# Queries and keys of the later pairs loaded in 32 by 32 blocks and turned by the vector engine instead of TensorE, in a fused attention and SwiGLU kernel

## The chip, the cores and the metric

One core of a Trainium2 chip; the four sets of experiments ran on four different chips, each with the kernel before beside it. The time is the device time of one execution in microseconds; quoted are medians of repeated runs with their lowest and highest. All runs of this study were in the fast state (granted TensorE clock 0.994 to 0.998 of full speed in the profiled ones). Profiled spans are some 2 us shorter than the times, and their sums are told as spans. One profile is of one run, and runs of one kernel differ by up to some 4 us, so differences of spans are checked against medians where it matters.

## The reference, cut to what matters

```python
# q, k, v: (8 batches, 12 heads, 448 tokens, 64 features), fp32
def rmsnorm(x, g):
    rms = np.sqrt(np.mean(x * x, axis=-1, keepdims=True) + 1e-06)
    return x / rms * g
q_n, k_n = rmsnorm(q, g_q), rmsnorm(k, g_k)
scores = np.matmul(q_n, k_n.transpose(0, 1, 3, 2)) / np.sqrt(64)
attn = softmax(scores)                          # rows of 448
out = np.matmul(attn, v)
# then (8*448, 768) tokens go through a SwiGLU block: w_gate, w_val 768x1536, w_out 1536x768
```

In both kernels the products of the scores take queries and keys with features on partitions. They come from memory with tokens first: somebody has to turn (transpose) them.

## The kernel before

Two heads make a pair; there are 48 pairs. Pairs 0 to 11 run first and are not touched. Pairs 12 to 47 are woven into the SwiGLU block's products in three stretches of twelve. Every piece of work is registered with an engine, an estimated duration, a wished time and its dependencies; a list scheduler then fixes the order of instructions of each engine. The timelines below show ScalarE in that order: in the changed kernel its exponentials start at 776.11 us, behind a copy that waits for the vector engine until 775.54 (3.4 us after TensorE's first scores of the pair; 2.6 us in e13, where that copy comes sooner). Pieces marked `port=True` are kept apart in the scheduler's plan; in the piece of code below these are the scalings and the additions of the sums, but not the power. The names of PSUM (where TensorE's results lie) and SBUF (the working memory) are used as in the code.

```python
BUFS = dict(qk=4, v=2, t=2, QT=2, KT=2, e=4, eh=2, ..., st=2, at=2, ss=3, rr=4, ...)   # cut

def attention(m):                    # one later pair
    # load: tokens on partitions, rows of 64 features (256 B), 8 issues a pair   (cut)
    def summed():                    # squares were made by ScalarE into t
        ss = take("ss", m, [P, 2 * 2 * NJ])
        nc.vector.tensor_reduce(out=ss, in_=..., axis=AX.X, op=ALU.add)   # 16 norms a partition
        nc.vector.tensor_scalar_add(ss, ss, D * 1e-6)
    def inverse():                   # 1/sqrt as a power, on GpSimd
        nc.gpsimd.tensor_tensor(out=rr, in0=tiles["ss", m], in1=minus_half, op=ALU.pow)
    # scale(x): t = qk * rr on GpSimd, once for queries and once for keys, port=True   (cut)
    def transpose():                 # 8 TensorE transposes into a PSUM tile
        ps = take("st", (m, "t"), [P, 2, TB])
        for x in range(2):
            for j in range(NJ):
                w = width(j)
                nc.tensor.transpose(ps[:, x, ds(P * j, w)], ..., ident[0:w, 0:w])
    def keys():                      # PSUM -> SBUF
        nc.scalar.copy(take("KT", m, [P, S]), tiles["st", (m, "t")][:, 1, 0:S])
    def queries():                   # PSUM -> SBUF, times both gains
        nc.vector.tensor_scalar(out=take("QT", m, [P, S]), in0=tiles["st", (m, "t")][:, 0, 0:S],
                                scalar1=gg, scalar2=None, op0=ALU.mult)
    # scores: QT, KT -> st;  exps on ScalarE: st -> e
    # sums of exps: two GpSimd additions (add_up 1, 2), then the last part on the vector engine:
    adds.append(add("DVE", 1.24, base + 6.0, lambda: add_up(3), after=[ex[3], adds[-1]], port=True, ...))
    # weighted sums (e, v -> at) and denominators (ones x sums -> st) on TensorE   (cut)
```

Of the kernel before, what the change touches and what calls it, by code (L numbers as in the profile page):

```python
# [9 lines left out]
F32 = mybir.dt.float32  # L10
# [459 lines left out]
def fast(  # L470
# [39 lines left out]
    P = 128  # L510
# [24 lines left out]
        qk=4, v=2, t=2, QT=2, KT=2, e=4, eh=2, sums=1, more=1, inv=1, rows=3, st=2, at=2, ss=3, rr=4,  # L535
# [41 lines left out]
    minus_half = const.tile([P, 2 * 2 * NJ], F32, name="minus_half")  # L577
# [36 lines left out]
    def first_attention(m):  # L614
# [57 lines left out]
        def inverse():  # L672
            rr = take("rr", m, [R, 2 * 2 * NJ])
            nc.gpsimd.tensor_tensor(
                out=rr,
                in0=tiles["ss", m],
                in1=minus_half[0:R],
                op=ALU.pow,
            )
# [178 lines left out]

    def width(j):
        return P if j < NJ - 1 else D  # L860

    def attention(m):
# [13 lines left out]
        def load(name, key, src, when):  # L876
            def emit():
                x = take(name, key, [P, NJ, 2, D])
                for h in range(2):
                    rows = src[b, 2 * c + h][0 : P * (NJ - 1)]  # L880
                    nc.sync.dma_start(x[:, 0 : NJ - 1, h], rows.rearrange("(j p) d -> p j d", p=P))
                rows = src[b][2 * c : 2 * c + 2, P * (NJ - 1) :].rearrange("h s d -> s h d")
                for p in (0, D):
                    nc.sync.dma_start(x[ds(p, D), NJ - 1], rows)

            return add("SP", 2.4, when, emit, takes=[(name, key)], kb=256, early=25.0)

        loaded = [load("qk", (m, x), src, ready - 26.0) for x, src in enumerate((q, k))]
        load_v = load("v", m, v, ready - 16.0)

        def square(x):
            if x == 0:
                take("t", m, [P, 2, NJ, 2, D])
            nc.scalar.activation(
                tiles["t", m][:, x].rearrange("p j h d -> p (j h d)"),
                tiles["qk", (m, x)].rearrange("p j h d -> p (j h d)"),
                AF.Square,
            )

        squares = []  # L900
        for x in range(2):
            squares.append(
                add(
                    "ACT", 0.6, ready - 15.0, lambda x=x: square(x),
                    after=[loaded[x], *squares], uses=[("qk", (m, x))] + [("t", m)] * x,
                    takes=[("t", m)] * (1 - x),
                )
            )

        def summed():  # L910
            ss = take("ss", m, [P, 2 * 2 * NJ])
            nc.vector.tensor_reduce(
                out=ss, in_=tiles["t", m].rearrange("p x j h d -> p (x j h) d"), axis=AX.X, op=ALU.add
            )
            nc.vector.tensor_scalar_add(ss, ss, D * 1e-6)  # L915

        sums = add(
            "DVE", 1.4, ready - 14.0, summed, after=squares, uses=[("t", m)], takes=[("ss", m)]
        )

        def inverse():
            rr = take("rr", m, [P, 2 * 2 * NJ])
            nc.gpsimd.tensor_tensor(out=rr, in0=tiles["ss", m], in1=minus_half, op=ALU.pow)  # L923

        rr = add(
            "POOL", 3.0, ready - 12.0, inverse, after=[sums], uses=[("ss", m)], takes=[("rr", m)]
        )

        def scale(x):
            rr = tiles["rr", m][:, ts(x, 2 * NJ)].rearrange("p (n one) -> p n one", one=1)  # L930
            nc.gpsimd.tensor_tensor(  # L931
                out=tiles["t", m][:, x].rearrange("p j h d -> p (j h) d"),
                in0=tiles["qk", (m, x)].rearrange("p j h d -> p (j h) d"),
                in1=rr.to_broadcast([P, 2 * NJ, D]),
# [5 lines left out]
                "POOL", 1.03, ready - 8.0, lambda x=x: scale(x), after=[rr], port=True,  # L940
                uses=[("qk", (m, x)), ("t", m), ("rr", m)],
            )
            for x in range(2)
# [3 lines left out]
        def transpose():  # L947
            ps = take("st", (m, "t"), [P, 2, TB])
            for x in range(2):
                for j in range(NJ):  # L950
                    w = width(j)
                    nc.tensor.transpose(  # L952
                        ps[:, x, ds(P * j, w)],
                        tiles["t", m][0:w, x, j].rearrange("p h d -> p (h d)"),
                        ident[0:w, 0:w],
                    )

        turned = add(
            "PE", 0.9, ready - 6.0, transpose, after=scaled, uses=[("t", m)],
            takes=[("st", (m, "t"))], mode="full",  # L960
        )

        def keys():
            nc.scalar.copy(take("KT", m, [P, S]), tiles["st", (m, "t")][:, 1, 0:S])  # L964

        def queries():
            nc.vector.tensor_scalar(  # L967
                out=take("QT", m, [P, S]), in0=tiles["st", (m, "t")][:, 0, 0:S], scalar1=gg,
                scalar2=None, op0=ALU.mult,
# [3 lines left out]
            "ACT", 0.53, ready - 5.0, keys, after=[turned], takes=[("KT", m)],  # L973
            uses=[("st", (m, "t"))],
        )
        qt = add(
            "DVE", 0.68, ready - 5.0, queries, after=[turned], takes=[("QT", m)],
            uses=[("st", (m, "t"))],
# [730 lines left out]
```

## Time and profile before

| | before |
|---|---|
| time, median of 3 runs | 1597.41 us (1596.78 to 1598.51) |
| profiled span | 1596.5 us |
| TensorE busy | 1558.7 us |
| vector, ScalarE, GpSimd busy | 864.6, 418.5, 661.9 us |
| denominator to denominator inside a stretch | 15.78 us |

The last row is the gauge that this document uses most. Each later pair has one burst on TensorE (scores, weighted sum, scores, denominator) and then matmuls of the SwiGLU block up to the next burst. The eight denominator matmuls (out st, in sums and ones) occur once a pair, so the distance between their starts is the pair's period. A pair whose period is well above the usual one is called late below. One caution: where the scheduler puts the denominators behind half of a product, one period is long and a later one short, and little is lost. The prediction shows the busy line, the chain and the main groups of this kernel.

One view that the prediction does not show: the chain of work near the end of the first stretch of the kernel before (start us, us, what).

```profile
495.39 0.54 ACT KT L964
...
495.95 0.70 DVE QT L967
...
496.69 0.98 PE st L989 x8
```

TensorE ended its turns (L952) at 495.37 and has no product left to put between them and the scores (L989), so the way through PSUM, copy of the keys and then the queries, lies on the chain: 496.69 - 495.37 = 1.32 us of it is not TensorE's.

### The profile page before, as it was taken

To read this page: it belongs to the slowest core of one execution; us is meant where nothing else is said; L and a number is where in the kernel's file an instruction comes from. 1 tells how busy PE (TensorE), PEld (TensorE's weight loads), DVE (VectorE), ACT (ScalarE), POOL (GpSimd) and SP (SyncE) were. 2 spreads that over 40 slices of the span, in tenths; PEclk is the share of its full clock that TensorE was granted. 3 is DMA by queue.
4 is the path that set the end of the run, shared out by engine and by line. 5 is a ranking of instruction groups with operands and counts; after the bars stand their busy time and mean duration, and the time that the engine had idled before them with its cause. 6 is when DMAs were issued, how large, how long until landed. Compare 5 with 4: busy or idle time off the path is not lost.

```text
span 1596.5 us, 17686 instructions
## 1 busy us (share of the span) xinstructions
PE 1558.7 (98%) x6672; PEld 778.3 (49%) x6672; DVE 864.6 (54%) x1017; ACT 418.5 (26%) x617; POOL 661.9 (41%) x440
## 2 busy tenths in 40 slices
PE   6998999999999999999999999999999999999998
PEld 2333544545454555544555455554545455555555
DVE  5989768775565434345556633444565563343221
ACT  6864333233332101122333200112333311000000
POOL 5881447564552322444554322344565331222000
PEclk9999999999999999999999999999999999999999
DMA  6655687643422113222333121332333211111232
GB/s 174 198 158 192 223 269 238 217 128 80 116 66 88 60 40 86 74 87 64 104 106 94 52 70 40 88 77 76 105 98 98 70 65 59 40 60 40 94 109 76
DMA packets 195012, 166.82 MB, mean 104 GB/s; under 512 B 132453, under 2 KB 184933, under 8 KB 194149
## 3 DMA queue, kind: packets, MB, share of 16 engines
q1 hardware_dynamic: 186304, 154.57, 32.3%
q10 hardware_dynamic: 8612, 11.02, 2.0%
q8 instruction: 55, 0.90, 0.2%
q14 instruction: 41, 0.33, 0.1%
HBM read 135.66 MB, written 29.88 MB: 104 GB/s over the span
## 4 chain that ended last, share of the span: by engine, by line
PE 77%; DVE 1%; ACT 1%; issue 0%; ACTq 0%
PE mm L1308 35%; PE mm L1489 25%; PE at L1058 6%; PE st L989 6%; PE st L952 3%; PE st L1071 2%; DVE gt L1420 0%; ACT es L1000 0%; DVE sums L1011 0%; DVE hs L1457 0%; DVE QT L967 0%; ACT wide L1413 0%; DVE gt L1457 0%; DVE s L1326 0%; ACT KT L964 0%
## 5 line engine op out<-in xcount | busy, mean ns | idle before, releaser
L1308 PE MATMUL mm<-xs,ws 128*128 128x448 f32 x2016 | 767.0, 542 | 7.4 <-DVE xs L1145 4.9
L1308 PEld LDWEIGHTS mm<-xs,ws 128*128 128x128 f32 x2016 | 381.9, 190 | 386.4 <-issue 370.9
L1292 POOL TENSOR_TENSOR ws<-ws 128x384 f32<-128x384 f32 x192 | 205.7, 1082 | 419.2 <-DMA ws<-quarters 314.6
L1489 PE MATMUL mm<-ws,gt 128*128 128x384 f32 x912 | 306.9, 491 | 0.0
L1489 PEld LDWEIGHTS mm<-ws,gt 128*128 128x128 f32 x912 | 169.6, 190 | 129.1 <-issue 16.9
L923 POOL TENSOR_TENSOR rr<-ss,minus_half 128x16 f32<-128x16 f32 x36 | 106.8, 2965 | 164.8 <-DVE ss L915 160.6
L1000 ACT ACTIVATE es<-st 128x896 f32<-128x896 f32 x108 | 95.2, 915 | 190.2 <-PE at L1058 141.1
L1005 POOL TENSOR_TENSOR sums<-es 128x896 f32<-128x896 f32 x36 | 76.0, 2112 | 156.6 <-ACT es L1000 120.7
L989 PE MATMUL st<-QT,KT 64*64 64x448 f32 (+1 forms) x1152 | 112.4, 501 | 5.5 <-DVE QT L967 3.5
L1326 DVE TENSOR_TENSOR s<-s,mm 128x448 f32<-128x448 f32 x96 | 59.6, 620 | 105.1 <-PE mm L1308 105.0
L1104 DVE RECIPROCAL inv<-inv 128x448 f32<-128x448 f32 x36 | 106.3, 2953 | 1.2
L1326 DVE TENSOR_TENSOR wide<-s,mm 128x448 f32<-128x448 f32 x72 | 44.7, 620 | 100.3 <-PE mm L1308 100.3
L1489 PE MATMUL mm<-ws,hs 128*128 128x384 f32 x288 | 97.2, 491 | 0.0
L1326 DVE TENSOR_TENSOR gt<-s,mm 128x448 f32<-128x448 f32 x72 | 44.6, 620 | 89.0 <-PE mm L1308 89.0
L1349 ACT COPY s<-mm 128x448 f32<-128x448 f32 x48 | 25.5, 532 | 246.5 <-PE mm L1308 246.5
L1058 PE MATMUL at<-es,v 64*64 64x448 f32 x864 | 89.5, 541 | 0.0
L1110 DVE TENSOR_TENSOR xs<-xs,at 128x448 f32<-128x448 f32 x36 | 22.3, 620 | 123.2 <-ACT xs L1107 123.2
L931 POOL TENSOR_TENSOR t<-qk,rr 128x512 f32<-128x512 f32 x72 | 86.2, 1218 | 2.5
L1413 ACT ACTIVATE wide<-gt 128x1344 f32<-128x1344 f32 x24 | 31.8, 1323 | 182.6 <-DVE gt L1326 182.6
L1005 POOL TENSOR_TENSOR sums<-sums,es 128x896 f32<-128x896 f32 x36 | 75.2, 2090 | 2.7
L1489 PEld LDWEIGHTS mm<-ws,hs 128*128 128x128 f32 x288 | 53.5, 190 | 40.9 <-issue 4.2
L1566 DVE TENSOR_TENSOR rows<-part,mm 128x384 f32<-128x384 f32 x56 | 30.9, 552 | 69.6 <-PE mm L1489 53.7
(93 smaller groups left out, 1374.9 us busy)
## 6 DMA issues: line engine op xcount, KB each, us to landing
ws<-quarters SPq DMA_DIRECT2D x48, 768.0 KB, 4.3
ws<-out_sides SPq DMA_DIRECT2D x28, 1152.0 KB, 6.2
out_sides<-hs SPq DMA_DIRECT2D x6, 1536.0 KB, 7.6
out_dram<-rows ACTq DMA_DIRECT2D x42, 192.0 KB, 1.9
stage<-in_moe_w_val_dram SPq DMA_DIRECT2D x10, 768.0 KB, 6.5
qk<-in_q_dram SPq DMA_DIRECT2D x72, 96.0 KB, 2.6
qk<-in_k_dram SPq DMA_DIRECT2D x72, 96.0 KB, 2.6
v<-in_v_dram SPq DMA_DIRECT2D x72, 96.0 KB, 2.5
```

The costliest lines, as they stand in the source:

```text
L923: nc.gpsimd.tensor_tensor(out=rr, in0=tiles["ss", m], in1=minus_half, op=ALU.pow)
L931: nc.gpsimd.tensor_tensor(out=tiles["t", m][:, x].rearrange("p j h d -> p (j h) d"), in0=tiles["qk", (m, x)].rearrange("p j h d -> p (j h) ...
L952: nc.tensor.transpose(ps[:, x, ds(P * j, w)], tiles["t", m][0:w, x, j].rearrange("p h d -> p (h d)"), ident[0:w, 0:w],)
L989: nc.tensor.matmul(st[ds(D * x, D), h, 0:n], tiles["KT", m][rows, ds(P * j + D * of_keys, D)], tiles["QT", m][rows, ds(Q * of_queries, n)] ...
L1000: nc.scalar.activation(e, tiles["st", (m, j)][:, :, 0 : S * width(j) // P], AF.Exp)
L1005: nc.gpsimd.tensor_tensor(out=to, in0=tiles["e", (m, 0)] if j == 1 else to, in1=e, op=ALU.add)
L1058: nc.tensor.matmul(tiles["at", (m, x)][ds(D * h, D), queries], tiles["v", m][rows, j, h], tiles["e", (m, j)][rows, h], start=j == 0, stop= ...
L1104: nc.vector.reciprocal(inv, inv)
L1292: lambda to=to, a=a, b=b: nc.gpsimd.tensor_tensor(out=tiles[key][:, to], in0=tiles[key][:, a], in1=tiles[key][:, b], op=ALU.subtract,),
L1308: nc.tensor.matmul(into[:, 0:S], w[:, side, c, :], xs[:, side, c], start=(fresh and c == 0), stop=(c == NK - 1), skip_group_check=not fina ...
L1326: nc.vector.tensor_tensor(out=to(), in0=one(), in1=two[:, 0:S], op=ALU.add)
L1489: nc.tensor.matmul(banks[bank][:, 0:HALF], of(g), w[:, ts(g, HALF)], start=(g == 0), stop=(g == NG - 1),)
```

## The change

The intent: take the transposes off TensorE, which is busy for 98% of the span, and give them to the vector engine, which is not. `nc.vector.transpose` is used block by block, 32 by 32: the load places each head's features in two halves of 32, in four partition groups, and each block is turned where it lies (128x448 took 0.62 to 0.64 us, and the result is correct). Each partition then holds half of each row's sum of squares; the halves are swapped by four small copies and added, and the power runs on 28 columns instead of 16.

```diff
-            # rows of 64 features, tokens on partitions
+                to = take("qk", (m, x), [P, NC, C])                  # C = 32, NC = 14
+                for g in range(P // C):
+                    rows = src[b, 2 * c + g // 2][:, ts(g % 2, C)]
+                    nc.sync.dma_start(to[ts(g, C)], rows.rearrange("(c i) f -> i c f", i=C))
...
-            nc.vector.tensor_scalar_add(ss, ss, D * 1e-6)
+        def swap():
+            for g in range(P // C):
+                nc.scalar.copy(ss[ts(g ^ 1, C), 1], ss[ts(g, C), 0])
+        def both():
+            nc.vector.scalar_tensor_tensor(
+                ss[:, 0], ss[:, 0], D * 1e-6, ss[:, 1], op0=ALU.add, op1=ALU.add)
...
-            nc.gpsimd.tensor_tensor(out=rr, in0=tiles["ss", m], in1=minus_half, op=ALU.pow)   # 16
+            nc.gpsimd.tensor_tensor(out=rr, in0=tiles["ss", m][:, 0], in1=minus_half, op=ALU.pow)  # 28
...
-        def transpose():   # 8 x nc.tensor.transpose into PSUM
-        def keys():        # ScalarE, PSUM -> KT
-        def queries():     # vector engine, PSUM -> QT, times gg
+        def transpose(x):
+            to = take("KT", m, [P, S]) if x else tiles["qk", (m, 0)]...
+            nc.vector.transpose(to, tiles["t", m][:, x]...)
+        def queries():
+            nc.scalar.activation(take("QT", m, [P, S]), tiles["qk", (m, 0)]..., AF.Copy, scale=gg)
```

Wished times and estimates of these pieces change with it (the load 2 us earlier, squares and reduction 3, the power 2, the scalings 1, keys before queries); `ss` has two buffers instead of three.

More of the change, by code (lines that the diff above doesn't have):

```diff
@@ L534, in fast @@
     BUFS = dict(
-        qk=4, v=2, t=2, QT=2, KT=2, e=4, eh=2, sums=1, more=1, inv=1, rows=3, st=2, at=2, ss=3, rr=4,
+        qk=4, v=2, t=2, QT=2, KT=2, e=4, eh=2, sums=1, more=1, inv=1, rows=3, st=2, at=2, ss=2, rr=4,
         ws=2, s1=1, s2=1, s3=1, wide=1, part=7,
@@ L576, in fast @@
     gg = const.tile([P, 1], F32, name="gg")
-    minus_half = const.tile([P, 2 * 2 * NJ], F32, name="minus_half")
+    minus_half = const.tile([P, 2 * S // 32], F32, name="minus_half")
     warm = const.tile([P, 1], F32, name="warm")
@@ L676, in inverse @@
                 in0=tiles["ss", m],
-                in1=minus_half[0:R],
+                in1=minus_half[0:R, 0 : 2 * 2 * NJ],
                 op=ALU.pow,
@@ L857, in first_attention @@
             sides(b // 2, c % NK, when + 6.0)
+    C = 32
+    NC = S // C
     def width(j):
@@ L874, in attention, with load, load_values @@
         add = order.add
-        def load(name, key, src, when):
+        def load(x, src):
             def emit():
-                x = take(name, key, [P, NJ, 2, D])
-                for h in range(2):
-                    rows = src[b, 2 * c + h][0 : P * (NJ - 1)]
-                    nc.sync.dma_start(x[:, 0 : NJ - 1, h], rows.rearrange("(j p) d -> p j d", p=P))
-                rows = src[b][2 * c : 2 * c + 2, P * (NJ - 1) :].rearrange("h s d -> s h d")
-                for p in (0, D):
-                    nc.sync.dma_start(x[ds(p, D), NJ - 1], rows)
-            return add("SP", 2.4, when, emit, takes=[(name, key)], kb=256, early=25.0)
-        loaded = [load("qk", (m, x), src, ready - 26.0) for x, src in enumerate((q, k))]
-        load_v = load("v", m, v, ready - 16.0)
+                to = take("qk", (m, x), [P, NC, C])
+                for g in range(P // C):
+                    rows = src[b, 2 * c + g // 2][:, ts(g % 2, C)]
+                    nc.sync.dma_start(to[ts(g, C)], rows.rearrange("(c i) f -> i c f", i=C))
+            return add("SP", 2.4, ready - 28.0, emit, takes=[("qk", (m, x))], kb=224, early=25.0)
+        loaded = [load(x, src) for x, src in enumerate((q, k))]
+        def load_values():
+            x = take("v", m, [P, NJ, 2, D])
+            for h in range(2):
+                rows = v[b, 2 * c + h][0 : P * (NJ - 1)]
+                nc.sync.dma_start(x[:, 0 : NJ - 1, h], rows.rearrange("(j p) d -> p j d", p=P))
+            rows = v[b][2 * c : 2 * c + 2, P * (NJ - 1) :].rearrange("h s d -> s h d")
+            for p in (0, D):
+                nc.sync.dma_start(x[ds(p, D), NJ - 1], rows)
+        load_v = add("SP", 2.4, ready - 16.0, load_values, takes=[("v", m)], kb=256, early=25.0)
         def square(x):
             if x == 0:
-                take("t", m, [P, 2, NJ, 2, D])
-            nc.scalar.activation(
-                tiles["t", m][:, x].rearrange("p j h d -> p (j h d)"),
-                tiles["qk", (m, x)].rearrange("p j h d -> p (j h d)"),
-                AF.Square,
-            )
+                take("t", m, [P, 2, NC, C])
+            nc.scalar.activation(tiles["t", m][:, x], tiles["qk", (m, x)], AF.Square)
         squares = []
@@ L903, in attention @@
                 add(
-                    "ACT", 0.6, ready - 15.0, lambda x=x: square(x),
+                    "ACT", 0.53, ready - 18.0, lambda x=x: square(x),
                     after=[loaded[x], *squares], uses=[("qk", (m, x))] + [("t", m)] * x,
@@ L910, in summed @@
         def summed():
-            ss = take("ss", m, [P, 2 * 2 * NJ])
             nc.vector.tensor_reduce(
-                out=ss, in_=tiles["t", m].rearrange("p x j h d -> p (x j h) d"), axis=AX.X, op=ALU.add
-            )
-            nc.vector.tensor_scalar_add(ss, ss, D * 1e-6)
+                out=take("ss", m, [P, 2, 2 * NC])[:, 0],
+                in_=tiles["t", m].rearrange("p x c f -> p (x c) f"),
+                axis=AX.X,
+                op=ALU.add,
+            )
+        def swap():
+            ss = tiles["ss", m]
+            for g in range(P // C):
+                nc.scalar.copy(ss[ts(g ^ 1, C), 1], ss[ts(g, C), 0])
@@ L917, in attention, with inverse @@
+        def both():
+            ss = tiles["ss", m]
+            nc.vector.scalar_tensor_tensor(
+                ss[:, 0], ss[:, 0], D * 1e-6, ss[:, 1], op0=ALU.add, op1=ALU.add
+            )
+        def inverse():
+            rr = take("rr", m, [P, 2 * NC])
+            nc.gpsimd.tensor_tensor(
+                out=rr, in0=tiles["ss", m][:, 0], in1=minus_half, op=ALU.pow
+            )
         sums = add(
-            "DVE", 1.4, ready - 14.0, summed, after=squares, uses=[("t", m)], takes=[("ss", m)]
+            "DVE", 1.1, ready - 17.0, summed, after=squares, uses=[("t", m)], takes=[("ss", m)]
@@ L919, in attention @@
         )
-        def inverse():
-            rr = take("rr", m, [P, 2 * 2 * NJ])
-            nc.gpsimd.tensor_tensor(out=rr, in0=tiles["ss", m], in1=minus_half, op=ALU.pow)
+        sums = add("ACT", 0.9, ready - 16.0, swap, after=[sums], uses=[("ss", m)])
+        sums = add("DVE", 0.15, ready - 15.0, both, after=[sums], uses=[("ss", m)])
         rr = add(
-            "POOL", 3.0, ready - 12.0, inverse, after=[sums], uses=[("ss", m)], takes=[("rr", m)]
+            "POOL", 5.2, ready - 14.0, inverse, after=[sums], uses=[("ss", m)], takes=[("rr", m)]
@@ L927, in attention @@
         )
         def scale(x):
-            rr = tiles["rr", m][:, ts(x, 2 * NJ)].rearrange("p (n one) -> p n one", one=1)
+            rr = tiles["rr", m][:, ts(x, NC)].rearrange("p (c one) -> p c one", one=1)
             nc.gpsimd.tensor_tensor(
-                out=tiles["t", m][:, x].rearrange("p j h d -> p (j h) d"),
-                in0=tiles["qk", (m, x)].rearrange("p j h d -> p (j h) d"),
-                in1=rr.to_broadcast([P, 2 * NJ, D]),
+                out=tiles["t", m][:, x], in0=tiles["qk", (m, x)], in1=rr.to_broadcast([P, NC, C]),
@@ L939, in attention @@
             add(
-                "POOL", 1.03, ready - 8.0, lambda x=x: scale(x), after=[rr], port=True,
+                "POOL", 1.0, ready - 9.0, lambda x=x: scale(x), after=[rr], port=True,
                 uses=[("qk", (m, x)), ("t", m), ("rr", m)],
             )
-            for x in range(2)
+            for x in (1, 0)
         ]
-        def transpose():
-            ps = take("st", (m, "t"), [P, 2, TB])
-            for x in range(2):
-                for j in range(NJ):
-                    w = width(j)
-                    nc.tensor.transpose(
-                        ps[:, x, ds(P * j, w)],
-                        tiles["t", m][0:w, x, j].rearrange("p h d -> p (h d)"),
-                        ident[0:w, 0:w],
-                    )
-        turned = add(
-            "PE", 0.9, ready - 6.0, transpose, after=scaled, uses=[("t", m)],
-            takes=[("st", (m, "t"))], mode="full",
-        )
-        def keys():
-            nc.scalar.copy(take("KT", m, [P, S]), tiles["st", (m, "t")][:, 1, 0:S])
+        def transpose(x):
+            to = take("KT", m, [P, S]) if x else tiles["qk", (m, 0)].rearrange("p c i -> p (c i)")
+            nc.vector.transpose(to, tiles["t", m][:, x].rearrange("p c f -> p (c f)"))
         def queries():
-            nc.vector.tensor_scalar(
-                out=take("QT", m, [P, S]), in0=tiles["st", (m, "t")][:, 0, 0:S], scalar1=gg,
-                scalar2=None, op0=ALU.mult,
+            nc.scalar.activation(
+                take("QT", m, [P, S]), tiles["qk", (m, 0)].rearrange("p c i -> p (c i)"), AF.Copy,
+                scale=gg,
             )
         kt = add(
-            "ACT", 0.53, ready - 5.0, keys, after=[turned], takes=[("KT", m)],
-            uses=[("st", (m, "t"))],
+            "DVE", 0.62, ready - 6.0, lambda: transpose(1), after=scaled[:1], takes=[("KT", m)],
+            uses=[("t", m)],
         )
         qt = add(
-            "DVE", 0.68, ready - 5.0, queries, after=[turned], takes=[("QT", m)],
-            uses=[("st", (m, "t"))],
+            "DVE", 0.62, ready - 6.0, lambda: transpose(0), after=scaled[1:],
+            uses=[("t", m), ("qk", (m, 0))],
+        )
+        qt = add(
+            "ACT", 0.53, ready - 5.0, queries, after=[qt], uses=[("qk", (m, 0))], takes=[("QT", m)]
         )
```

## The prediction

> **What bounds the kernel now.** I read the busy shares of the page first, then the chain of work that ended last, then the groups by line and shape, the waits, and a timeline of one pair.
>
> ```profile
> PE 1558.7 (98%) x6672; PEld 778.3 (49%) x6672; DVE 864.6 (54%) x1017; ACT 418.5 (26%) x617; POOL 661.9 (41%) x440
> ```
>
> TensorE is busy for 98% of the span and no other engine for more than 54%. A busy PE may still hide waits, so the chain decides. Two pieces of it, the first inside a stretch where attention of later pairs is woven into the down projection (columns: start us, us, what), the second where two products stand side by side:
>
> ```profile
> 416.64 1.66 PE st L989 x16
> 418.30 2.63 PE at L1058 x32
> 420.94 1.13 PE st L989 x16
> 422.07 0.03 issue
> 422.09 0.98 PE st L1071 x8
> 423.08 4.07 PE mm L1489 x12
> 427.14 1.21 PE st L952 x8
> 428.35 4.07 PE mm L1489 x12
> 432.42 1.66 PE st L989 x16
> ...
> 871.36 7.94 PE mm L1489 x24
> ```
>
> The chain runs through PE alone: scores, weighted sum, scores, denominator, product, **transposes (L952, 1.21 us)**, product, and round again. One pair takes 432.42 - 416.64 = 15.78 us, and 0.03 us of it is not PE work. So whatever leaves PE here shortens the kernel, until another engine's own cycle per pair becomes longer than PE's. There are 36 such pairs (12 to 47, in three stretches of about 240 us each); pairs 0 to 11 and the pure up projection are not touched.
>
> The groups that matter (line, engine, operation, tiles, shapes, count | busy us, mean ns of one | idle before):
>
> ```profile
> L923 POOL TENSOR_TENSOR rr<-ss,minus_half 128x16 f32<-128x16 f32 x36 | 106.8, 2965 | 164.8 <-DVE ss L915 160.6
> L931 POOL TENSOR_TENSOR t<-qk,rr 128x512 f32<-128x512 f32 x72 | 86.2, 1218 | 2.5
> L964 ACT COPY KT<-st 128x448 f32<-128x448 f32 x36 | 19.2, 532 | 173.6 <-PE st L952 173.6
> L967 DVE TENSOR_SCALAR QT<-st,gg 128x448 f32<-128x448 f32 x36 | 24.5, 681 | 20.4 <-ACT KT L964 20.3
> L912 DVE TENSOR_REDUCE ss<-t 128x16 f32<-128x1024 f32 x36 | 43.7, 1214 | 4.1 <-ACT t L894 3.9
> ```
>
> The power on POOL costs 2.97 us for 16 columns, POOL idles before it, and the other engines mostly wait for PE.
>
> [...]each of four partition groups takes one head and half of its features. [...]the trace has 620 to 622 ns for L1110[...]. [...]I therefore **estimate** 0.62 us for one 128x448 transpose. No run yet shows it.
>
> [...](start, us, engine, line):
>
> ```profile
> 801.11 2.91 POOL L923 TENSOR_TENSOR rr<-ss,minus_half 128x16 f32<-128x16 f32 x1 [4.24 <-DVE ss L915]
> 802.30 2.55 DVE L1457 TENSOR_TENSOR gt<-gt,hs 128x2304 f32<-128x2304 f32 x1
> 804.10 2.65 POOL L931 TENSOR_TENSOR t<-qk,rr 128x512 f32<-128x512 f32 x2
> ```
>
> The two scalings are stretched from 2.05 to 2.65 us behind a vector operation, but the power did not hold that vector operation up. So a longer power should not lock the vector engine out.
>
> [...]Here 256 B rows land in 2.3 to 2.6 us, issued far ahead, and the DMA share in these stretches is 0.29.
>
> **The change, part by part** (per later pair unless said).
> 1. Removed from PE: 8 transposes, 1.21 us of the chain. Also a restart: two separate products of 12 cost 2 x 4.07 = 8.14, a joined run of 24 costs 7.94, so each break costs 0.20 us. The built order has 76 runs of product matmuls before and 47 after, 29 fewer. Total: 36 x 1.21 + 29 x 0.20 = 43.6 + 5.8 = **49.4 us**, all on the chain. The pair's cycle becomes 15.78 - 1.41 = 14.37 us.
> 2. Vector engine: adds two transposes (2 x 0.62) and one small add (about 0.2); loses QT from PSUM (0.68) and a small add (0.21); the sum over 896 instead of 1024 columns saves 0.13. Net +0.4 us, beside PE.
> 3. ScalarE: the KT copy is replaced by scaling QT (about the same 0.53 to 0.6); four 32x28 copies that swap the halves' sums. A one-column ACT operation costs 203 ns in this trace, so about 4 x 0.23 = 0.9 us. Squares are 0.15 shorter. Net +0.8 us, from 5.7 busy in 15.8.
> 4. POOL: the power on 28 columns. A POOL memset of 16 columns costs 112 ns, so I take (2912 - 112) / 16 = 175 ns a column, and 28 x 175 + 112 = 5.0 us, +2.1. Scalings on 448 columns: -0.3. Net +1.8 us: 9.1 to 9.7 busy of 15.8 becomes about 11.3 of 14.4.
> 5. Loads: 2 x 1792 packets of 128 B instead of 2 x 1024 of 256 B, so 55,296 more over the kernel (195,012 to about 250,300), 8 issues as before. Hidden.
> 6. PSUM tile st is taken five times a pair instead of six: looser.
>
> So the sum is 1597.4 - 49.4 = 1548 us if nothing new enters the chain.
>
> **What could enter it.** With the built order of each engine I followed two loops through one cycle. In the first stretch: small add 0.2, power 5.0, two scalings 1.8, QT transpose 0.62, then denominator add, reciprocal, division, sums and PSUM read on the vector engine (439.48 to 445.49 in the trace, 6.0 us), back to the small add: 13.6, plus four handovers of some 0.08 = **13.9 us against 14.37**. In the later stretches: small add 0.2, power 5.0, two sums of exponentials 4.2, sums 1.24, PSUM read 0.55, reduction 1.07, swap 0.9, five handovers 0.4 = 13.6. Both fit, with only 0.5 to 0.8 us to spare. QT's scaling stands just before the exponentials in ScalarE's order in many pairs; it must wait for the scores that free its buffer (1.7 us into the burst) and ends near 2.5, while the exponentials could not start before 2.6 anyway (in the trace they wait for the weighted sum). Where the up projection and attention meet, vector transposes waiting on POOL stand in front of PSUM reads that PE needs every 2.3 us; I allow 3 us in all for that. Prediction: **1551 us**.
>
> **Rivals.**
> - *A POOL and vector loop becomes the bound.* If the transpose costs twice my estimate, or the power 6 us, the first loop comes to 14.5 to 15.1, and in the 30 or so affected pairs 0.2 to 0.7 us are lost: 6 to 20 us, giving 1555 to 1570. For it: little slack, in-order queues. Against it: every term but two was measured in this trace.
> - *Packets of 128 B arrive late or delay the weights on the same rings.* Against it: DMA share 0.29, loads two pairs ahead; the late one would show as ACT squares waiting for qk. Some risk only in the first up projection, where the share is 0.76. Cost up to 5 us.
> - *The full gain, even without the 3 us of losses:* 1546 to 1548, for which the small waits in today's mixed stretches (L989 on QT, 3.5 us) would have to go too.
> - *No gain*, because ScalarE's swap or QT stalls each burst by 1.2 us or more. The timing above speaks against it; it would give 1590 or more.
>
> **Range and chances.** 8 in 10: 1542 to 1566. 2% faster means under about 1565.5, so losses must stay under 17 us of 49. I give faster 0.84, within 2% 0.15, slower 0.01.
>
> **What would show it right or wrong.** Right: no PE transposes in the groups; PE busy near 1505 to 1510; in the chain 7.94 us runs of 24 between bursts; bursts 14.4 us apart in all three stretches; transposes of 0.62 us; power about 5.0 us; POOL near 725 us. Wrong: PE idle before L999 (scores) charged to QT or KT, before L1499 charged to vector PSUM reads, or ACT's exponentials starting later than 2.6 us into the burst; a spacing of bursts over 14.6 us; squares waiting for qk loads.

## The result, and the profile after

The result is correct. The time is **1550.41 us** (1549.68 to 1550.64, 4 runs) against 1597.15 us (1596.78 to 1598.51, 4 runs) of the kernel before in the same rounds. The ratio is 0.9705, 95% interval 0.9688 to 0.9722: faster. A ratio is the mean time of one kernel's fast runs over that of the other's fast runs of the same rounds, so it is not quite the ratio of the medians. Repeated later without an edit, the changed kernel took 1549.69 us, ratio 0.9698.

The page of the kernel after:

```profile
PE 1507.7 (97%) x6384; PEld 742.4 (48%) x6384; DVE 892.6 (58%) x1053; ACT 449.6 (29%) x761; POOL 726.4 (47%) x440
```

TensorE lost 288 instructions (36 pairs of 8) and 51.0 us; the span lost 1596.5 - 1547.9 = 48.6. It is still the only engine above 60%.

Its chain in the first stretch shows the intended picture: scores, weighted sum, then one unbroken run of 24 product matmuls, and no turns between.

```profile
383.01 7.94 PE mm L1499 x24
390.95 1.66 PE st L999 x16
...
397.30 7.94 PE mm L1499 x24
405.23 1.66 PE st L999 x16
```

405.23 - 390.95 = 14.28 us a pair, where it was 15.78. The new and changed groups (columns as in the prediction):

```profile
L940 POOL TENSOR_TENSOR rr<-ss,minus_half 128x28 f32<-128x28 f32 x36 | 179.8, 4996 | 122.8 <-DVE ss L934 122.8
...
L974 ACT ACTIVATE QT<-qk,gg 128x448 f32<-128x448 f32 x36 | 24.1, 670 | 43.3 <-DVE qk L971 34.4 <-PE st L999 8.7
L971 DVE STREAM_TRANSPOSE KT<-t 128x448 f32<-128x448 f32 x36 | 23.0, 638 | 25.2 <-PE st L999 21.3 <-POOL t L955 3.9
L1021 DVE TENSOR_TENSOR sums<-sums,more 64x448 f32<-64x448 f32 x72 | 61.9, 860 | 0.9
```

A vector turn takes 0.62 (queries) and 0.64 us (keys) in the mean, the power 4.81 us in the median. The last line is an instruction that the change did not touch: the last part of the sums. It went from a mean of 702 ns before to 860, with a median of 622. Something stretches it in some pairs.

The period is not 14.28 everywhere. In the second stretch it is 14.92 for three pairs running, in the third 15.98, 14.92 and 15.08; single ones stand near the ends (15.04 and 14.71 in stretch 1, 15.22 in 2, 16.41 in 3). The chain of one of the three:

```profile
772.74 1.66 PE st L999 x16
774.40 1.55 PE at L1068 x16
...
776.11 1.71 ACT es L1010 x2
...
777.87 0.98 PE st L999 x8
778.85 0.87 PE st L1081 x8
```

The chain leaves TensorE here: scores, half of the weighted sum, then the exponentials on ScalarE, for which the next scores wait. They start 776.11 - 772.74 = 3.4 us into the burst. The timeline of the same pair says why (start us, us, engine, line, operation; in brackets the idle time before it and who ended it):

```profile
769.76 2.61 POOL L955 TENSOR_TENSOR t<-qk,rr 128x448 f32<-128x448 f32 x2
770.21 2.64 DVE L1021 TENSOR_TENSOR sums<-sums,more 64x448 f32<-64x448 f32 x2
...
773.35 1.08 DVE L920 TENSOR_REDUCE ss<-t 128x28 f32<-128x896 f32 x1
...
774.46 0.88 ACT L930 COPY ss<-ss 32x28 f32<-32x28 f32 x4 [4.92 <-DVE ss L920]
774.80 0.64 DVE L971 STREAM_TRANSPOSE qk<-t 128x448 f32<-128x448 f32 x1
...
775.54 0.67 ACT L974 ACTIVATE QT<-qk,gg 128x448 f32<-128x448 f32 x1 [0.19 <-DVE qk L971]
775.64 4.81 POOL L940 TENSOR_TENSOR rr<-ss,minus_half 128x28 f32<-128x28 f32 x1 [3.28 <-DVE ss L934]
...
776.11 1.70 ACT L1010 ACTIVATE es<-st 128x896 f32<-128x896 f32 x2
```

ScalarE's order puts the scaled copy of the queries (L974) ahead of the exponentials (L1010). The copy waits for the turn of the queries (L971), and the turn stands behind the last additions of the sums (L1021) and the reduction (L920) in the vector engine's order. The four swap copies (L930), which wait for the same reduction, stand before it on ScalarE too and end at 775.34, only 0.1 us before the turn: reduction and turn together would have to come earlier. The two additions, 1.24 us in all when alone, take 2.64 beside the two scalings on GpSimd. The scalings are stretched as well: 1.32 and 1.33 us here, 0.94 in the median. That each stretches the other is called blocking below. In such pairs one power starts 14.91 us after the other (760.73, 775.64): power 4.81, two GpSimd sums, the vector additions, PSUM read, reduction, swap, small add, and the next power.

The longest period of this kind, 15.98, has one more stretched term, seen in the lines of the third stretch:

```profile
1142.62 2.55 DVE L1467 TENSOR_TENSOR gt<-gt,hs 128x2304 f32<-128x2304 f32 x1
1142.79 7.05 POOL L940 TENSOR_TENSOR rr<-ss,minus_half 128x28 f32<-128x28 f32 x1 [4.46 <-DVE ss L934]
```

This power began 0.17 us after a vector product with two SBUF inputs and took 7.05 us instead of 4.81; the next power starts 17.6 us after it, and the two additions between them are stretched too (2.64 us at 1154.50). The same happens once in the first stretch (at 404.19), where no pair becomes late. By itself it makes no pair late in stretch 3 either: in e13 below the power there still takes 7.05 us, and the period is 14.37.

Adding up the profiled spans by parts shows where time came from and went. A part's end is the start of a denominator product; e1 is the first experiment below.

| part, us | before | after | e1: no turns at all |
|---|---|---|---|
| start to the first denominators of stretch 1 | 353.6 | 345.4 | 347.4 |
| stretch 1 | 172.4 | 162.3 | 159.4 |
| up projection between | 214.3 | 209.3 | 209.3 |
| stretch 2 | 170.9 | 159.9 | 157.0 |
| up projection between | 214.3 | 209.3 | 209.3 |
| stretch 3 | 170.9 | 161.5 | 157.1 |
| the rest | 300.2 | 300.3 | 300.4 |
| span | 1596.5 | 1547.9 | 1539.8 |

Against a kernel with no turns at all, the change loses 0.9 us up to the end of stretch 1, 2.9 in stretch 2 and 4.3 in stretch 3: 8.1 us in all, and nothing in the rest. By the medians it is 1550.41 - 1543.02 = 7.4 us. The first row alone is not firm: among runs with the changed kernel's order it lies between 345.0 and 347.6.

### The profile page after: what moved, and what is told of

It reads as the page before. It is cut to its first block, busy times and chain, and to the rows that moved or that the text cites. A ratio compares the mean times of both kernels' runs of the same rounds, so it can differ in the third digit from the quotient of the medians.

```text
span 1547.9 us, 17349 instructions
## 1 busy us (share of the span) xinstructions
PE 1507.7 (97%) x6384; PEld 742.4 (48%) x6384; DVE 892.6 (58%) x1053; ACT 449.6 (29%) x761; POOL 726.4 (47%) x440
## 2 busy tenths in 40 slices
DMA packets 250307, 164.43 MB, mean 106 GB/s; under 512 B 187749, under 2 KB 240229, under 8 KB 249445
## 4 chain that ended last, share of the span: by engine, by line
PE 73%; DVE 2%; ACT 1%; DMA 0%; issue 0%; SPq 0%; ACTq 0%; DVEq 0%
PE mm L1318 37%; PE mm L1499 24%; PE st L999 5%; PE at L1068 5%; PE st L1081 2%; ACT es L1010 1%; DVE hs L1467 0%; DMA ws<-out_sides 0%; DVE inv L1114 0%; DVE gt L1467 0%; DVE xs L1155 0%; SPq L886 0%; DVE sums L1021 0%; DVE rows L1576 0%; DVE xs L1123 0%
## 5 line engine op out<-in xcount | busy, mean ns | idle before, releaser
L1499 PE MATMUL mm<-ws,gt 128*128 128x384 f32 x912 | 302.6, 489 | 0.0
L940 POOL TENSOR_TENSOR rr<-ss,minus_half 128x28 f32<-128x28 f32 x36 | 179.8, 4996 | 122.8 <-DVE ss L934 122.8
L1010 ACT ACTIVATE es<-st 128x896 f32<-128x896 f32 x108 | 95.2, 914 | 137.7 <-PE at L1068 63.2
L955 POOL TENSOR_TENSOR t<-qk,rr 128x448 f32<-128x448 f32 x72 | 78.0, 1104 | 1.3
```

Source lines behind the costliest of these rows:

```text
L940: nc.gpsimd.tensor_tensor(out=rr, in0=tiles["ss", m][:, 0], in1=minus_half, op=ALU.pow)
L955: nc.gpsimd.tensor_tensor(out=tiles["t", m][:, x], in0=tiles["qk", (m, x)], in1=rr.to_broadcast([P, NC, C]), op=ALU.mult,)
L1010: nc.scalar.activation(e, tiles["st", (m, j)][:, :, 0 : S * width(j) // P], AF.Exp)
L1499: nc.tensor.matmul(banks[bank][:, 0:HALF], of(g), w[:, ts(g, HALF)], start=(g == 0), stop=(g == NG - 1),)
```

## The experiments

Before ran beside each set: 1597.59 us for the first four, 1597.82 for the next four, 1597.27 for e11 and e12, 1597.38 for the last two.

**e1: what the turns cost at most.** The kernel before without its TensorE transposes; keys and queries are copied from the scaled rows as they lie, wrong on purpose.

```diff
-        def transpose():  ...  nc.tensor.transpose(...)
+        def straight(x):
+            return tiles["t", m][:, x].rearrange("p j h d -> p (j h d)")[:, 0:S]
...                                      # queries likewise, from straight(0)
-            nc.scalar.copy(take("KT", m, [P, S]), tiles["st", (m, "t")][:, 1, 0:S])
+            nc.scalar.copy(take("KT", m, [P, S]), straight(1))
```

> The kernel before with its TensorE transposes taken out and nothing put in their place (keys and queries are copied from the scaled rows as they lie, so the result is wrong on purpose). Theory A, that the gain is TensorE time and its restarts: 1541 to 1549 us (1597 less 49.4, less some 4 us for the short chain transposes, KT, QT at the end of each stretch). Rival B, that the gain comes from the other loads or from other waits: 1580 us or more. If A holds, the distance to the changed kernel's 1550.4 is what the new path costs.

Measured: 1543.02 us (1541.65 to 1544.18), ratio 0.966. The period is 14.28 us in nearly every pair. The span fell by 1596.5 - 1539.8 = 56.7 us, but the profiled run of e1 is the fastest of its four and that of the kernel before one of its slower ones (1598.39 us). By the medians of the same rounds it is 1597.59 - 1543.02 = 54.6 us. Either is more than the 49.4 that the prediction had worked out for the removal.

**e2: the turns put back.** The changed kernel with eight unread TensorE transposes per later pair, correct result.

```diff
+        def turns_again():
+            ps = take("st", (m, "t"), [P, 2, TB])
+            for x in range(2):
+                for j in range(NJ):
+                    w = width(j)
+                    nc.tensor.transpose(ps[:, x, ds(P * j, w)], ident[0:w, :], ident[0:w, 0:w])
+        add("PE", 0.9, ready - 6.0, turns_again, after=scaled, takes=[("st", (m, "t"))], mode="full")
```

> The changed kernel with eight TensorE transposes of the identity put back for each later pair, at the place where the kernel before had them; nobody reads them. Theory A: 1596 to 1604 us, all of the gain gone. Rival B: below 1570 us.

Measured: 1592.47 us (1591.80 to 1593.07), ratio 0.9967: below the expected range, but most of the gain is gone. Its chain in the first stretch:

```profile
404.90 1.21 PE st L978 x8
406.11 4.07 PE mm L1510 x12
```

The turns are back at 1.21 us, and the product is broken in two again. In stretches 2 and 3 the period is 15.69, and 15.69 - 14.28 = 1.41 us is the prediction's figure for turns and restart. Two things are seen in the rest. The late pairs are gone there: the seven full periods of each lie within 0.01 of 15.69, which fits a norm loop of 14.9 us that does not show under it. (In the first stretch e2 has late pairs of its own: 18.42, 17.69, 17.63.) And not all of the kernel before came back: stretches 2 and 3 take 169.4 us against 170.9 before, each up projection 213.5 against 214.3. Unrounded, that is 1.5 + 1.5 + 0.7 + 0.7 = 4.4 us of the kernel before that TensorE's work on turns does not account for. In a stretch, 0.75 of it is the pair with the way through PSUM (16.24 before, 15.49 in e2). In an up projection it is not that way: 0.49 us is a wait of TensorE for a vector read of PSUM (L1326, at 724.13) that e2 does not have.

**e3: half the power.** The changed kernel with the power on 14 columns, used for queries and keys alike, wrong on purpose, order of all engines unchanged.

```diff
-            rr = take("rr", m, [P, 2 * NC])
+            rr = take("rr", m, [P, 2 * NC])[:, 0:NC]
-                out=rr, in0=tiles["ss", m][:, 0], in1=minus_half, op=ALU.pow
+                out=rr, in0=tiles["ss", m][:, 0, 0:NC], in1=minus_half[:, 0:NC], op=ALU.pow
```

> The changed kernel with the power on 14 columns instead of 28 (keys use the queries' norms, wrong on purpose), the order of all engines unchanged. Theory C, that in about nine pairs POOL and the vector engine bind in turn (bursts 14.9 us apart instead of 14.28): the power falls from 4.8 to about 2.5 us, the late bursts come back to 14.28 and the time falls by 4 to 9 us, to 1541 to 1546. Rival D, that these bursts are late because ScalarE scales QT in front of the exponentials, whatever POOL does, or because of loads: 1549 to 1551 us.

Measured: 1545.03 us (1543.56 to 1546.39), ratio 0.9669. The power's median fell from 4.81 to 2.60 us, and the periods of 14.92 fell to 14.38 to 14.41, the 15.98 of stretch 3 to 14.49. So these late pairs hang on the loop in which the power lies; those near the ends of stretches 1 and 3 stayed (15.01, 14.77, 16.41). What it does not say is whether the power's length or something else in the loop is to blame.

**e4: large packets.** The changed kernel with loads in rows of 1792 B instead of 128 B, wrong data on purpose.

```diff
-                    rows = src[b, 2 * c + g // 2][:, ts(g % 2, C)]
-                    nc.sync.dma_start(to[ts(g, C)], rows.rearrange("(c i) f -> i c f", i=C))
+                    rows = src[b, 2 * c + g // 2][ts(g % 2, S // 2)]
+                    nc.sync.dma_start(to[ts(g, C)].rearrange("p c f -> p (c f)"),
+                                      rows.rearrange("(i c) f -> i (c f)", i=C))
```

> The changed kernel with the same bytes loaded in rows of 1792 B instead of 128 B (wrong data on purpose), as many transfers and the same places in the order. About 120,000 packets fewer of 250,307. Theory A: 1549 to 1551 us, the packets are hidden. Rival E, that late small packets cost time: 1547 us or less.

Measured: 1550.05 us (1549.28 to 1551.70), ratio 0.9702. The packets fell from 250,307 to 130,499 and the median time from issue to landing from 3.0 to 2.5 us (queries) and 2.5 to 2.0 (keys), but the periods stayed. The small rows cost nothing here.

**e6, e8, e10: three reorderings.** All keep the work and the result. e6 gives the scheduler the measured durations of the new pieces as estimates; e8 asks for the norms 30 us earlier; e10 does both.

```diff
-        rr = add("POOL", 5.2, ready - 14.0, inverse, ...)      # after
+        rr = add("POOL", 4.85, ready - 14.0, inverse, ...)     # e6, and five more estimates alike
+        rr = add("POOL", 5.2, ready - 44.0, inverse, ...)      # e8, with squares, reduction, swap, add
```

> The changed kernel with the scheduler's cost estimates of the new small operations set to what the trace after measured (squares 0.58, scaled copy of the queries 0.70, power 4.85, small add 0.2, vector turns 0.66); same work and a correct result, other order on each engine. Theory C (what is left between 1550.4 and 1545 is eight late pairs, whose norm loop stands badly in the order): an order made with true durations might take some of them away, 1545 to 1551. Rival (the late pairs come from vector and GpSimd work blocking each other, which the scheduler does not know of): the late spacings move to other pairs, and the time stays at 1549 to 1553. A guess towards the rival: 1550.

> The changed kernel with the chain of norms (squares, reduction, swap copies, small adds, power) asked for 30 us earlier, so that the reduction stands ahead of the divide and adds of the vector engine where it can; same work, correct. Theory C: the power is then ready well before the scaled rows are wanted, the late pairs shrink, 1545 to 1549. Rival (buffers of the rows limit how early it can go, so the order changes without effect, or the earlier norms hold up the eviction of TensorE's results): 1549 to 1556.

> The two last edits together: measured durations as estimates, and norms 30 us earlier; same work, correct. Theory C: 1545 to 1549. Rival: 1549 to 1556. Whichever of the two alone is faster, this one should be no more than 3 us from it.

Measured: e6 1553.07 us (1552.38 to 1555.11), e8 1555.84 us (1555.64 to 1557.23), e10 1556.41 us (1554.18 to 1556.82). All are a little slower than the changed kernel, but not for one reason. In e6 late pairs appeared in the first stretch as well (16.46, 14.92, 16.18), which fits its rival; the time is just above both ranges. (The scheduler does know of the blocking, by `port=True`, against the words of that expectation. Its plan keeps additions and scalings apart; on the chip they met, as at 769.76 and 770.21 above.) In e8 and e10 the loss is not in the stretches: these take 161.3, 160.1, 161.1 us in e8 and 164.0, 158.7, 158.7 in e10, against 162.3, 159.9, 161.5. But the first denominators come at 351.9 and 353.6 us instead of 345.4, and in front of them TensorE has one long wait for a vector read of PSUM (e8; 5.36 us in e10, 1.64 in the changed kernel):

```profile
338.60 11.98 PE L1318 MATMUL mm<-xs,ws 128*128 128x448 f32 x24 [5.35 <-DVE s L1336]
```

So the reading of TensorE's results is held up, as the rival of e8 said, though not by norms directly: in front of that read the vector engine works through additions of the SwiGLU block (L1467), which take 1.2 to 2.5 us each beside GpSimd's work instead of 0.55 (in the changed kernel too: 1.18 to 2.44 us from 331.73 to 340.1, beside sums and scalings). This wait explains 3.7 of the 6.5 us in front; the rest stays open. The theory that earlier norms shrink the late pairs held in part, in stretches 2 and 3 of e10 (4.0 us less together); more was lost in front. e10 is 3.3 us from e6, just outside the 3 us expected.

**e7: how much slack the loop has.** The changed kernel with an unread power on 8 columns after each power.

```diff
+            nc.gpsimd.tensor_tensor(
+                out=spare_power, in0=tiles["ss", m][:, 0, 0:8], in1=minus_half[:, 0:8], op=ALU.pow)
```

> The changed kernel with one more power per later pair on the GpSimd engine, on 8 columns, its result unread, order unchanged: some 1.5 us more in the norm loop (0.158 us for each column, from 2.91 us at 16 and 4.81 at 28, gives 1.3 us, and a start of each). It measures how much slack the loop had. Theory C (the loop of norms took 13.6 to 13.9 us beside TensorE's 14.28 in most pairs, so 0.4 to 0.7 us of slack): spacing goes to 14.9 to 15.4 in most pairs and to about 16.4 in the late ones, 1572 to 1592 in all. Rival (the loop has 1.5 us of slack or more in most pairs, the eight late pairs are a thing of their own): most pairs stay at 14.28, only the eight late ones grow, 1553 to 1566.

Measured: 1573.09 us (1572.11 to 1574.09), ratio 0.9847. The extra power took 1.64 us in the median, and GpSimd's timeline in the second stretch shows the loop by itself:

```profile
785.08 4.81 POOL L941 TENSOR_TENSOR rr<-ss,minus_half 128x28 f32<-128x28 f32 x1 [3.27 <-DVE ss L935]
...
801.45 4.81 POOL L941 TENSOR_TENSOR rr<-ss,minus_half 128x28 f32<-128x28 f32 x1 [3.27 <-DVE ss L935]
```

801.45 - 785.08 = 16.37 us, where the changed kernel had 14.91: there the loop was already the bound, and the added time came through almost whole. In the first stretch four of seven powers come 14.97 to 15.00 us apart, which less 1.64 is 13.35 us for the loop without the addition: it fits under 14.28 with 0.9 us to spare. The changed kernel agrees: after its stretched power of the first stretch the next two distances, 13.49 and 13.63 us, are below TensorE's period. The expectation for single pairs failed, though: four periods of the first stretch stay at 14.23 to 14.28. Norms are made ahead, and it seems that this lead is used up first (not tested); then come 17.86 and 17.26. The time agreed with theory C, the picture in single pairs only in part.

**e12: the addition without its second input.** The vector engine's last addition replaced by a copy with one input, wrong on purpose, order unchanged. This was to take the blocking away; that one input would do so was my assumption, and no run had shown it.

```diff
-                    nc.vector.tensor_tensor(out=part, in0=part, in1=e[ds(D * x, D)], op=ALU.add)
+                    nc.vector.tensor_scalar(part, e[ds(D * x, D)], 1.0, None, op0=ALU.mult)
```

> The changed kernel with the vector engine's last addition of the sums replaced by a copy with one input, in the same place of the order, wrong on purpose: it takes the blocking away and shortens nothing else. Theory D: the instruction falls from 0.86 us to below 0.5, the GpSimd scaling beside it from 1.3 to some 1.05, and the 14.92 spacings fall to 14.3 to 14.5: 1545 to 1548.5 in all. Rival (the power's length alone makes the late pairs): they stay near 14.9, and the time at 1549 to 1551.

Measured: 1543.97 us (1543.89 to 1544.85), ratio 0.9668; the periods of 14.92 in stretch 2 are gone (14.28 to 14.44 in their place); in stretch 3 the 15.98 only fell to 15.28, and the power before it still took 7.05 us. But the blocking was not taken away, and the mean of the instruction fell to 0.63 us, not below 0.5. The timeline of e12:

```profile
768.83 2.37 POOL L955 TENSOR_TENSOR t<-qk,rr 128x448 f32<-128x448 f32 x2
769.28 2.18 DVE L1021 TENSOR_SCALAR sums<-more 64x448 f32<-64x448 f32 x2
```

Alone, a copy takes 391 ns in the median; here two take 2.18 us. The copy is stretched beside the scalings as the addition was, so the assumption did not hold here. So e12 shows that 0.46 us less in this place (2.64 to 2.18) is enough to free the late pairs of stretch 2, where the loop was only some 0.6 us too long (14.91 against 14.28). It refutes the rival that only the power's length makes them, but it does not show what happens without blocking.

**e11 and e13: only the order of that addition.** The changed kernel with one constraint: for some pairs the last addition must come after the turn of the queries that stands in the same period. e11 does so for seven pairs in each of stretches 2 and 3, e13 for three and four.

```diff
+    add3 = {}                                        # last addition of each pair
+    turned_first = {29: 26, 30: 27, 31: 28, 41: 39, 42: 40, 43: 41, 44: 42}       # e13
...
+        if m in turned_first:
+            add3[turned_first[m]]["after"].append(qt)     # qt: the vector engine's turn of pair m
```

> The changed kernel with one order constraint: in the second and third stretch, for seven pairs each, the vector engine's last addition of the sums comes after the turn of the queries that stands in the same period (before, it stood ahead of reduction, eviction and turn). Same work, correct result. Theory D (the late pairs are queueing: the scaled copy of the queries stands in the scalar engine's queue ahead of the exponentials, waits for the turn, and the turn waits behind the addition, which takes 2.64 us instead of 1.24 because it and the scaling on GpSimd block each other): the spacing of 14.92 in the second stretch goes to 14.3 to 14.5, and some of the third stretch's late ones too, 1545 to 1548.5. Rival (the order is not what makes them late, or what moves back costs as much): 1549 to 1555, as the three other reorderings did.

> As the version with the turn ahead of the last addition, but for three pairs of the second stretch and four of the third alone, to avoid the new late pair (18.35 us) that came with the seventh. Same work, correct. Theory D: 1544 to 1547, no spacing near 18 in the second stretch. Rival (each reordering only moves the late pairs): 1547 to 1551.

> The changed kernel once more, without an edit, in the same rounds as the next run, so that the better version has a partner: 1549 to 1552, ratio 0.9695 to 0.9715. If it falls to 1547 or below, the gain of the reordered versions is within what chips and rounds differ by.

Measured: e11 1546.15 us (1544.89 to 1547.08), ratio 0.9681, correct. The 14.92 became 14.37, but one new period of 18.35 us came up. It is not a late pair: in the chain there (814 to 829 us) TensorE does not wait, the denominators stand behind half of a product, and the next two periods are 14.48 and 10.84. e13 leaves it out: **1544.62 us** (1544.55 to 1546.22), ratio 0.9672, correct, against 1549.69 us (1548.26 to 1550.64) for the changed kernel in the same rounds. The timeline of e13 at the place shown above for the changed kernel:

```profile
770.09 2.23 POOL L958 TENSOR_TENSOR t<-qk,rr 128x448 f32<-128x448 f32 x2
770.54 1.07 DVE L923 TENSOR_REDUCE ss<-t 128x28 f32<-128x896 f32 x1
...
772.29 1.73 PE L1004 MATMUL st<-QT,KT 64*64 64x448 f32 x16
...
772.87 0.64 DVE L974 STREAM_TRANSPOSE qk<-t 128x448 f32<-128x448 f32 x1
773.43 1.21 DVE L1026 TENSOR_TENSOR sums<-sums,more 64x448 f32<-64x448 f32 x2
...
774.90 1.73 ACT L1015 ACTIVATE es<-st 128x896 f32<-128x896 f32 x2
```

The reduction now runs beside the scalings, the turn follows, and the additions come after both and take 1.21 us for the two. The exponentials start 774.90 - 772.29 = 2.6 us into the burst, not 3.4. The period there is 14.37. The order change moves reduction, swap and turn forward together, so it does not say which of them counts most. Stretch 2 takes 157.2 us instead of 159.9, stretch 3 158.9 instead of 161.5; the other parts differ by under 0.7 us from the changed kernel's. This is the best correct version, 5.1 us under the changed kernel by the medians of the same rounds.

Not run, so not shown: a third buffer for the rows `t`, the power on the vector engine, rows of 64 B. There is no e5 or e9 among the runs.

## Why the prediction was right

The time of 1551 against 1550.41 measured is right, and so is the mechanism: TensorE bounds the kernel, what leaves its chain is gained, and one spare engine pays. How close the number came is partly luck, as the second and third points show. By its own steps:

- **TensorE as the bound.** Right. TensorE's busy time fell to 1507.7 us (predicted 1505 to 1510), runs of 24 at 7.94 us stand in the chain, and e2 gives 1.41 us per pair back.
- **The size of the removal, 49.4 us.** Too small by 5.2 us: e1 shows 54.6 by medians (56.7 between two single profiles). The step that failed is part 1, which counted TensorE's own work alone. In stretches 2 and 3 and the up projections between, e2 against before shows 4.4 us more than that work. Three sources are to be seen: the way through PSUM, which lay on the chain where no product covered it, 0.09 us in each pair's period (15.78 to 15.69), and TensorE's wait for a vector read of PSUM in each up projection. The first stretch I cannot divide, since e2 has late pairs of its own there.
- **The losses, 3 us.** Too small by 4.4 us (7.4 by medians against e1), and put in another place: they were allowed for where the up projection and attention meet, but up to the end of stretch 1 only 0.9 us was lost and in the up projections nothing; 7.2 us lie inside stretches 2 and 3. This miss and the one before nearly cancel. That is luck.
- **The second loop, 13.6 us for the later stretches.** This is the failed step. It was 14.91 us (power to power) in stretch 2. The main mis-sized term is the last addition of the sums, taken as 1.24 us, the time it has alone; it took 2.64 because the scalings stood beside it. The prediction asked only whether a power holds up the vector engine. The reverse happened as well: one power of stretch 3, behind a vector product, took 7.05 us, and its loop 17.6. In stretch 2, e12 and e13, which shorten or move this one instruction, remove the late pairs; e3 removes them by shortening another term of the loop.
- **The first loop, 13.9 us.** Close: 13.35 us by e7.
- **ScalarE's copy of the queries, harmless since it ends 2.5 us into the burst.** Right in most pairs. In the late ones it began 2.8 us into the burst and the exponentials 3.4 us into it. This is the sign "exponentials later than 2.6 us" that the prediction named. Two more of its signs of being wrong came up: periods over 14.6, and squares waiting for loads (57.2 us of ScalarE's idle time in 28 places, 11.5 in 4 before). With large packets these waits are 42.8 us in 25 places and the time is the same, so they are not what the packets' size would cost.
- **Costs of single pieces.** Transpose 0.62, an estimate that no run had shown, 0.62 to 0.64 measured; power 5.0, median 4.81; swap copies 0.23 each, 0.212; packets 250,300, 250,307; GpSimd 725, 726.4. Scaling QT was put at 0.53 to 0.6 and took 0.67. Two slips of the working changed nothing: a power of 6 us makes the first loop 14.9, not up to 15.1 (with the slow transpose too, 15.5), and the DMA share in the stretches reads 0.31 to 0.33, not 0.29.
- **Rivals.** The loop rival came true in a small number of pairs, and through pieces that stretch each other (2.64 us instead of 1.24) rather than through the durations it named. The packets were refuted (e4), and a loss of the whole gain did not happen. What stays open: why some pairs near the ends of stretches are late (14.71 in stretch 1, 16.41 in stretch 3). The 15.04 beside the first is no price of the new path, since e1 has it too (14.99). No reordering tried takes all of them away.

## What to carry to other kernels

When work leaves the bounding engine, count also what other engines did in series with it and only showed where nothing covered them; here the removal was worth about a tenth more than that engine's own time. The price of moving work was less in the added durations, which TensorE's period covered in most pairs, than in the order: a short instruction, which took 2.64 us instead of 1.24 beside the other engine's scalings, stood ahead of something that the bound engine needs, and moving it in seven pairs won back 5.1 of the some 7 us that the new path cost. Before taking a loop as slack, put into it the durations that its terms have beside their neighbours, not alone; and if such an instruction is not needed soon, order it after the one that is.

## What single pieces cost in these runs

- Vector and GpSimd work beside each other: for multiplications and sums both were stretched. In the changed kernel (769.76 and 770.21) the additions took 1.25 and 1.35 us and the scalings 1.32 and 1.33, alone 0.62 and 0.94. With the power on GpSimd the stretch was seen one way only. A vector product with two SBUF inputs that started 0.40 us after a power (at 776.04 in the changed kernel) took 2.52 us, no more than elsewhere (2.52 to 2.55), and the power stayed at 4.81. A power that started 0.17 us after such a product took 7.05 us (the lines at 1142.62 above).
- A power on GpSimd: over 128 partitions the medians were 1.64 us for 8 columns (e7), 2.60 for 14 (e3), 2.91 for 16 (before) and 4.81 for 28 (after): 0.158 us a column and some 0.38 us beside.
- The vector engine's turn: in fp32, 128x448 in blocks of 32 takes 0.62 to 0.64 us.
- Small packets: the loads here took 0.5 us longer to land in rows of 128 B than of 1792 B, but 120,000 packets fewer left the time at 1550.05 against 1550.41 us (e4).
- Breaking a run of matmuls on TensorE by matmuls of another kind: two products of 12 took 8.14 us, one of 24 took 7.94, so 0.20 us.
